# Layer 1 of the first mixture: both parts of the rows in one matmul of 448 columns, halves added on VectorE, ReLU and low part one block later

## The chip, the cores and the metric

The kernel runs on one core of a Trainium2 chip. The metric is the device time of one execution in microseconds (us). The kernel before took 871.7 us (median of 3 runs, 871.54 to 873.64).

## The reference

Attention over 4 batches, 12 heads, 448 positions and 64 dimensions gives 1792 rows of 768 numbers. Two mixtures of experts follow. The first gives each of its 8 experts exactly 224 rows; the second routes each row to its best expert with a gate weight.

```python
def _moe_ref(x, w_gate, w1, w2):
    N, D = x.shape                      # 1792, 768
    E = w_gate.shape[1]                 # 8 experts
    cap = N // E                        # 224 rows for each
    logits = x @ w_gate
    ...                                 # greedy assignment, best scores first, until an expert is full
    for e in range(E):
        mask = assigned == e
        h = np.maximum(x[mask] @ w1[e], 0.0)   # layer 1: 768 -> 1024
        out[mask] = h @ w2[e]                  # layer 2: 1024 -> 768
    return out
# the second mixture: e_idx = argmax(logits + bias of the row's modality),
# out[mask] = gate_w[mask, None] * (relu(x[mask] @ w1[e]) @ w2[e])
```

## The kernel before

All work is written out for one core in a fixed order: the instructions of each engine run in the order in which the program emits them, and semaphores make one engine wait for another. Attention fills about the first 245 us of the trace, the assignment of the first mixture the stretch up to about 290 us, and the experts the rest.

The experts are handled as tiles `u`. Tiles 0 to 7 are the experts of the first mixture, each 224 rows (two groups of 112). Tiles 8 and up belong to the second mixture, with 256 rows each (or 128 in a short one). Each matrix product is done in three parts so that rounded operands keep their accuracy: weights and rows are each split into an upper part and a low part (`wh`, `wl`, and `x[:, 0]`, `x[:, 1]`), and wh times upper, wh times low and wl times upper are summed in PSUM.

A tile is 16 chunks (`chunk(u, c)`). Chunks 0 to 7 are the 8 blocks of layer 1, 128 hidden units each: 6 slices of 128 input dimensions, and for each slice the three matmuls L1143 to L1145 of 224 columns, into one of three PSUM buffers `ph`. `layer1_end` then makes the ReLU on ScalarE (L1163, `hh`) and the low part on VectorE (L1164, `hl`), both from `ph`. Chunks 8 to 15 are layer 2 (L1177 to L1179, 384 columns each): chunk 8 uses blocks 0 to 3 of `hh` and `hl`, chunk 9 blocks 4 to 7, and so on for four outputs. A chunk has 12 of these matmuls; block 7 is first used by its 10th to 12th matmul in chunk 9, the 22nd to 24th of layer 2.

Within a chunk the order is: the matmuls of the layer; then what `run` finds in a table of work booked for that chunk (`at`); then the end of the layer; then work booked as late. Booked in the chunks of a tile of the first mixture are, among others:

- chunks 0 to 7: one slice each of the split of this tile's second weights (L815 on ScalarE makes the upper part, L817 on VectorE the low part, `w2s`, 768 columns);
- chunks 8 to 11: the splits of the next tile's first weights (`w1s`, 1024 columns), of which two stand in chunk 8, one in 9, two in 10 and one in 11;
- chunks 10 to 15: the transposes of the next tile's rows (L1120 to L1122);
- the routing of the tile before for the second mixture: transposes in chunks 0 and 1, logits in 2 (L1299, L1302), their sum in 3 (L1308, L1309), the choice in 4 (late, L1317 to L1323, six VectorE instructions and one of ScalarE), the placing in 6 (L1329 to L1345).

Tile 1 also has, in chunk 3, the sum of the lists of rows (L1254 to L1256), which waits for a load that follows a chain of scattering DMAs issued by GpSimd.

Of the kernel before, what the change touches and what calls it, by code (L numbers as in the profile page):

```python
# [8 lines left out]
FT = mybir.dt.float32  # L9
FR = mybir.dt.float32r  # L10
# [17 lines left out]
def build(ctx, tc, q, k, v, g_q, g_k, m1_gate, m1_w1, m1_w2, modality, m2_gate, m2_bias, m2_w1, m2_w2,  # L28
          out):
    nc = tc.nc  # L30
# [7 lines left out]
    E = m1_gate.shape[1]  # L38
    DJ = HD // 128
    F = m1_w1.shape[2]  # L40
    FB = F // 128
# [3 lines left out]
    T = 256  # L45
# [978 lines left out]
    with tc.If(f1 > 0):  # L1024
# [5 lines left out]
        with tc.If(f2 > 0):  # L1030
# [7 lines left out]
            with tc.If(f3 > 0):  # L1038
# [12 lines left out]
                hs = rr.tile([P, E], HF, name="hs")  # L1051
# [41 lines left out]


    act = ctx.enter_context(tc.tile_pool(name="act", bufs=1))
    HH, PY, LT2 = {}, {}, {}
    SHORT = set()
    bg = {}

# [3 lines left out]
    def run(w, late=False):  # L1103
        while bg.get((w, late)):
            f, a = bg[w, late].pop(0)
            f(*a)

    def shape(u):

        return (P, 2) if u < E else (128, 1) if u in SHORT else (128, 2)  # L1110
# [12 lines left out]

    def layer1(u, f):

        w, nt = shape(u)
        n = w * nt
        ph = ps1.tile([128, 512], FT, name="ph")
        o = slice(128 * f, 128 * f + 128)
        for j in range(DJ):  # L1130
            wh, wl = (W1S[u][:, i, j, o] for i in range(2))
            x = XS[u][:, j, :, :n]
            a, z = j == 0, j == DJ - 1
            if u == 0 and f == 0:

                for i in range(2):
                    nc.tensor.matmul(ph[:, :n], wh, x[:, i], start=(a and i == 0), stop=False)
                if z:
                    for k in range(DJ):
                        nc.tensor.matmul(ph[:, :n], W1S[u][:, 1, k, o], XS[u][:, k, 0, :n], start=False,  # L1140
                                         stop=(k == DJ - 1))
            elif nt == 2:
                nc.tensor.matmul(ph[:, :n], wh, x[:, 0], start=a, stop=False)  # L1143
                nc.tensor.matmul(ph[:, :n], wh, x[:, 1], start=False, stop=False)  # L1144
                nc.tensor.matmul(ph[:, :n], wl, x[:, 0], start=False, stop=z)  # L1145
            else:
                both = ph[:, :2 * n].rearrange("p (a n) -> p a n", a=2)
                nc.tensor.matmul(both, wh, x, start=a, stop=False)
                nc.tensor.matmul(both, wl, x, start=False, stop=z)
        return ph  # L1150

    def layer1_end(u, f, ph):
        w, nt = shape(u)
        n = w * nt
        if f == 0:
            HH[u] = [act.tile([128, FB, T], FR, name=nm) for nm in ("hh", "hl")]
        hh, hl = (x[:, f, :n] for x in HH[u])
        src = ph[:, :n]
        if nt == 1:
            src = act.tile([128, 128], FT, name="hs", bufs=2)  # L1160
            nc.scalar.activation(src, ph[:, n:2 * n], AF.Copy)
            nc.vector.tensor_add(src, ph[:, :n], src)
        nc.scalar.activation(hh, src, AF.Relu)  # L1163
        nc.vector.scalar_tensor_tensor(hl, src, 0.0, hh.bitcast(FT), op0=OP.max, op1=OP.subtract)  # L1164

    def layer2(u, i):
        w = shape(u)[0]
        t, s, z = i // 4, i // 2 % 2, i % 2
        if z == 0:
            PY[u] = ps2.tile([128, 512], FT, name="py")  # L1170
        hh, hl = HH[u]
        py = PY[u][:w, :384]
        o = slice(384 * s, 384 * s + 384)
        for f in range(4 * z, 4 * z + 4):
            wh, wl = (W2S[u][:, i, f, o] for i in range(2))
            a, b_ = (x[:, f, w * t:w * t + w] for x in (hh, hl))
            nc.tensor.matmul(py, a, wh, start=(f == 0), stop=False)  # L1177
            nc.tensor.matmul(py, b_, wh, start=False, stop=False)  # L1178
            nc.tensor.matmul(py, a, wl, start=False, stop=(f == FB - 1))  # L1179
# [20 lines left out]
    def chunk(u, c):  # L1200
        two = c >= 8 and c < 8 + 4 * shape(u)[1]
        if c < 8:
            ph = layer1(u, c)
        elif two:
            layer2(u, c - 8)
        run(16 * u + c)
        if c < 8:
            layer1_end(u, c, ph)
        elif two and c % 2:
            layer2_end(u, c - 8)  # L1210
        run(16 * u + c, True)

# [152 lines left out]
    took, cl, st, nt, ns, te, tb, one = (tq[:, i] for i in range(8))  # L1365
# [102 lines left out]
    for u in range(US):  # L1468
# [3 lines left out]
        for p in range(3, 7):  # L1472
            for i in range(2):
                c = 2 * (p - 3) + i
# [54 lines left out]
    for u in range(US):  # L1529
        for c in range(16):  # L1530
            chunk(u, c)
# [46 lines left out]
```

## Time and profile before

| | |
|---|---|
| median of 3 runs | 871.7 us (871.54 to 873.64) |
| the profiled execution | 873.17 us |
| its span, first to last instruction | 871.4 us |
| PE busy | 794.0 us, 91% of the span |
| VectorE (DVE) busy | 570.0 us, 65% |
| ScalarE (ACT) busy | 465.6 us, 53% |
| mean granted TensorE clock | 0.962 |

Times in the rows are microseconds from the start of the span. An instruction that overlaps its successor is counted at its full length in a mean, so the time from one start to the next (called a slot here) is shorter than the mean length: a row of the timeline gives a start, a length, and in brackets how long the engine was idle before it and who ended that. A granted clock of 1.00 is 2.4 GHz, 0.50 is 1.2 GHz.

The steady tiles of the first mixture are tiles 2 to 7; tile 2 starts layer 1 at about 371 us and layer 2 at 387.99 us.

### The profile page before, as it was taken

How to read it: one execution, taken by the hardware profiler on the slowest of the kernel's cores; microseconds unless marked ns; L12 is line 12 of the kernel's file. 1: busy time of each engine (PE TensorE's matmuls, PEld its weight loads, DVE VectorE, ACT ScalarE, POOL GpSimd, SP SyncE). 2: the span in 40 equal slices, each digit the busy share in tenths (PEclk: the TensorE clock that was granted, in tenths of full speed). 3: DMA queues.
4: the chain of work that ended last, by engine and by line, in shares of the span. 5: the costliest groups of instructions: out<-in, count | busy, mean ns of one | idle time of the engine just before them, and what ended most of it. 6: DMA issues, size and time to landing. Idle time of an engine off the chain costs nothing.

```text
span 871.4 us, 14927 instructions
## 1 busy us (share of the span) xinstructions
PE 794.0 (91%) x5630; PEld 653.5 (75%) x5630; DVE 570.0 (65%) x1196; ACT 465.6 (53%) x803; POOL 141.3 (16%) x230
## 2 busy tenths in 40 slices
PE   1589999999954998999999999999999999999994
PEld 1233333333343798999999999999999999999983
DVE  4899899894488954564746648475874565655641
ACT  3667767574361354554645546455564564555641
POOL 4440000000021344211101122121212010110000
PEclk9989999999965999999999999999999999999997
DMA  7349969774170695766757666485675775855710
GB/s 182 99 76 199 214 154 207 180 166 94 42 259 18 194 281 135 227 199 204 257 169 234 196 206 219 156 290 180 202 264 205 239 243 186 296 188 195 275 53 19
DMA packets 113785, 161.22 MB, mean 185 GB/s; under 512 B 59328, under 2 KB 77248, under 8 KB 113696
## 3 DMA queue, kind: packets, MB, share of 16 engines
q1 hardware_dynamic: 108928, 143.07, 55.7%
q0 software_dynamic: 4768, 17.02, 5.8%
q8 instruction: 49, 0.80, 0.4%
q14 instruction: 40, 0.33, 0.1%
HBM read 128.78 MB, written 17.22 MB: 168 GB/s over the span
## 4 chain that ended last, share of the span: by engine, by line
PE 52%; DMA 6%; issue 5%; DVE 1%; POOL 1%; SPq 0%; ACT 0%; POOLq 0%; DVEq 0%
PE py L1177 8%; PE py L1179 8%; PE py L1178 8%; PE ph L1143 8%; PE ph L1144 8%; PE ph L1145 8%; DMA l_d<-tok,p3i 4%; PE pt L1120 2%; DMA out_dram<-yr,lt 1%; PE pt L1289 1%; PE pi L1299 1%; DMA l<-l_d 1%; DMA lt<-l_d 0%; DVE w2s L817 0%; SPq L1250 0%
## 5 line engine op out<-in xcount | busy, mean ns | idle before, releaser
L1143 PE MATMUL ph<-xs,w1s 128*128 128x224 f32 (+1 forms) x714 | 201.4, 282 | 0.0
L1144 PE MATMUL ph<-xs,w1s 128*128 128x224 f32 (+1 forms) x714 | 197.1, 276 | 0.0
L1145 PE MATMUL ph<-xs,w1s 128*128 128x224 f32 (+1 forms) x714 | 197.0, 276 | 0.0
L1177 PE MATMUL py<-w2s,hh 128*112 128x384 f32 (+1 forms) x496 | 174.0, 351 | 1.4 <-ACT hh L1163 1.3
L1178 PE MATMUL py<-w2s,hl 128*112 128x384 f32 (+1 forms) x496 | 168.0, 339 | 0.0
L1179 PE MATMUL py<-w2s,hh 128*112 128x384 f32 (+1 forms) x496 | 167.9, 339 | 0.0
L817 DVE TENSOR_TENSOR w2s<-raw,w2s 128x768 fp32r<-128x768 f32 x128 | 122.5, 957 | 66.7 <-ACT w2s L815 66.6
L1143 PEld LDWEIGHTS ph<-xs,w1s 128*128 128x128 f32 x714 | 136.0, 190 | 2.9 <-DVE hl L1164 2.9
L1145 PEld LDWEIGHTS ph<-xs,w1s 128*128 128x128 f32 x714 | 136.2, 191 | 0.0
L1144 PEld LDWEIGHTS ph<-xs,w1s 128*128 128x128 f32 x714 | 136.2, 191 | 0.0
L817 DVE TENSOR_TENSOR w1s<-raw,w1s 128x1024 fp32r<-128x1024 f32 x96 | 113.3, 1221 | 16.4 <-ACT w1s L815 16.0
L815 ACT ACTIVATE w2s<-raw 128x768 fp32r<-128x768 f32 x128 | 107.3, 838 | 0.0
L1122 DVE TENSOR_TENSOR xs<-pt,xs 128x224 fp32r<-128x224 f32 (+2 forms) x92 | 36.6, 398 | 105.2 <-ACT xs L1121 105.2
L815 ACT ACTIVATE w1s<-raw 128x1024 fp32r<-128x1024 f32 x96 | 96.6, 1058 | 3.1 <-DVE lo L881 1.7
L1121 ACT ACTIVATE xs<-pt 128x224 fp32r<-128x224 f32 (+2 forms) x92 | 33.3, 362 | 112.5 <-PE pt L1120 86.6
L1177 PEld LDWEIGHTS py<-w2s,hh 128*112 128x112 f32 (+1 forms) x496 | 90.7, 183 | 2.3 <-ACT hh L1163 2.1
L438 ACT ACTIVATE pp<-sc,gs 128x896 f32<-128x896 f32 x72 | 70.0, 1006 | 41.1 <-PE sc L431 40.8
L1178 PEld LDWEIGHTS py<-w2s,hl 128*112 128x112 f32 (+1 forms) x496 | 90.8, 183 | 0.4
L1179 PEld LDWEIGHTS py<-w2s,hh 128*112 128x112 f32 (+1 forms) x496 | 90.4, 182 | 0.1
L1163 ACT ACTIVATE hh<-ph 128x224 fp32r<-128x224 f32 (+1 forms) x120 | 44.2, 368 | 78.6 <-PE ph L1145 76.2
L453 PE MATMUL av<-pp,vt 128*64 128x448 f32 x288 | 64.4, 554 | 0.0
L431 PE MATMUL sc<-qT,kT 128*128 128x448 f16 x144 | 53.1, 369 | 7.9 <-DVE qT L415 4.9
(321 smaller groups left out, 1087.0 us busy)
## 6 DMA issues: line engine op xcount, KB each, us to landing
raw<-in_moe_w_dram SPq DMA_DIRECT2D x48, 1024.0 KB, 4.9
raw<-in_moe_w_dram SPq DMA_DIRECT2D x64, 768.0 KB, 5.6
y_d<-yr SPq DMA_DIRECT2D x16, 336.0 KB, 3.8
qt<-in_q_dram SPq DMA_DIRECT2D x11, 448.0 KB, 5.2
kt<-in_k_dram SPq DMA_DIRECT2D x24, 192.0 KB, 3.6
vt<-in_v_dram SPq DMA_DIRECT2D x12, 384.0 KB, 4.5
qTs<-qT SPq DMA_DIRECT2D x20, 224.0 KB, 3.5
x_d<-xr SPq DMA_DIRECT2D x12, 336.0 KB, 3.0
```

The source lines that it names most:

```text
L431: nc.tensor.matmul(ps[:, s, :S], kT[:, 7 * j + 3 * s + g, :], rhs[s][z], start=(z == 0), stop=(z == 1))
L438: nc.scalar.activation(PP[n][:, 2 * g:2 * g + 2, :] if g < 3 else P7[n], ps[:, :w, :S], AF.Exp, scale=gs[:, 4:5])
L453: nc.tensor.matmul(AV[n][64 * s:64 * s + 64, :S], LV[u][:, 3 * (2 * j + s) + g, :], pp[:, 2 * g + s, :], start=(g == 0), stop=False, skip_ ...
L815: nc.scalar.activation(d[:, 0, j, c], RAW[u, p][:, i, c], AF.Copy)
L817: eng.tensor_sub(d[:, 1, j, c], RAW[u, p][:, i, c], d[:, 0, j, c].bitcast(FT))
L1143: nc.tensor.matmul(ph[:, :n], wh, x[:, 0], start=a, stop=False)
L1144: nc.tensor.matmul(ph[:, :n], wh, x[:, 1], start=False, stop=False)
L1145: nc.tensor.matmul(ph[:, :n], wl, x[:, 0], start=False, stop=z)
L1163: nc.scalar.activation(hh, src, AF.Relu)
L1177: nc.tensor.matmul(py, a, wh, start=(f == 0), stop=False)
L1178: nc.tensor.matmul(py, b_, wh, start=False, stop=False)
L1179: nc.tensor.matmul(py, a, wl, start=False, stop=(f == FB - 1))
```

## The change

For tiles of the first mixture (`u < E`) the two matmuls with the upper weights, which streamed 224 columns each into the same 224 columns of PSUM, become one that streams 448 columns into both halves of the buffer; the matmul with the low weights adds into the first half. The two halves then have to be added: ScalarE copies the second half into a new tile `hsum`, and VectorE adds the first half to it (`layer1_sum`). ReLU and low part read `hsum` in place of `ph`, and they are emitted one chunk later than before, ahead of the sum of the chunk's own block. The end of block 7 is thereby emitted in chunk 8. Tiles of the second mixture keep their order; a short one uses `hsum` where it had `hs`.

```diff
@@ layer1
             if u == 0 and f == 0:
-                for i in range(2):
-                    nc.tensor.matmul(ph[:, :n], wh, x[:, i], start=(a and i == 0), stop=False)
+                nc.tensor.matmul(ph[:, :2 * n].rearrange("p (a n) -> p a n", a=2), wh, x, start=a, stop=False,
+                                 skip_group_check=True)
...
+            elif u < E:
+                nc.tensor.matmul(ph[:, :2 * n].rearrange("p (a n) -> p a n", a=2), wh, x, start=a, stop=False,
+                                 skip_group_check=True)
+                nc.tensor.matmul(ph[:, :n], wl, x[:, 0], start=False, stop=z, skip_group_check=True)
             elif nt == 2:
@@ the end of a block
-    def layer1_end(u, f, ph):
+    def layer1_sum(u, f, ph):
...
         src = ph[:, :n]
-        if nt == 1:
-            src = act.tile([128, 128], FT, name="hs", bufs=2)
+        if u < E or nt == 1:
+            src = act.tile([128, T], FT, name="hsum", bufs=3)[:, :n]
             nc.scalar.activation(src, ph[:, n:2 * n], AF.Copy)
             nc.vector.tensor_add(src, ph[:, :n], src)
+        return src
+
+    def layer1_end(u, f, src):
+        w, nt = shape(u)
+        n = w * nt
+        hh, hl = (x[:, f, :n] for x in HH[u])
         nc.scalar.activation(hh, src, AF.Relu)
         nc.vector.scalar_tensor_tensor(hl, src, 0.0, hh.bitcast(FT), op0=OP.max, op1=OP.subtract)
@@ chunk
         run(16 * u + c)
-        if c < 8:
-            layer1_end(u, c, ph)
-        elif two and c % 2:
+        if u < E:
+            if 0 < c < 9:
+                layer1_end(u, c - 1, HS.pop())
+            if c < 8:
+                HS.append(layer1_sum(u, c, ph))
+        elif c < 8:
+            layer1_end(u, c, layer1_sum(u, c, ph))
+        if two and c % 2:
             layer2_end(u, c - 8)
```

On VectorE, around the end of layer 1 of a tile, the program before has this order (chunks 6 to 11; `w2s` and `w1s` are the low parts of weights, `hl` the low parts of blocks 6 and 7):

```order
L817 TENSOR_TENSOR w2s<-raw,w2s 128x768
L1164 SCALAR_TENSOR_TENSOR hl<-ph,hh 128x224
L817 TENSOR_TENSOR w2s<-raw,w2s 128x768
L1164 SCALAR_TENSOR_TENSOR hl<-ph,hh 128x224
L817 TENSOR_TENSOR w1s<-raw,w1s 128x1024 x5
```

The changed program has this there (L1175 is the low part, of blocks 5, 6 and 7, L1167 the sum of the halves, of blocks 6 and 7):

```order
L817 TENSOR_TENSOR w2s<-raw,w2s 128x768
L1175 SCALAR_TENSOR_TENSOR hl<-hsum,hh 128x224
L1167 TENSOR_TENSOR hsum<-ph,hsum 128x224
L817 TENSOR_TENSOR w2s<-raw,w2s 128x768
L1175 SCALAR_TENSOR_TENSOR hl<-hsum,hh 128x224
L1167 TENSOR_TENSOR hsum<-ph,hsum 128x224
L817 TENSOR_TENSOR w1s<-raw,w1s 128x1024 x2
L1175 SCALAR_TENSOR_TENSOR hl<-hsum,hh 128x224
L817 TENSOR_TENSOR w1s<-raw,w1s 128x1024 x3
```

The low part of block 7 has moved behind two splits of the next tile's first weights, and each block has one instruction more. On ScalarE the program before has, in chunks 6 to 9:

```order
L815 ACTIVATE w2s<-raw 128x768
L1163 ACTIVATE hh<-ph 128x224
L815 ACTIVATE w2s<-raw 128x768
L1163 ACTIVATE hh<-ph 128x224
L815 ACTIVATE w1s<-raw 128x1024 x3
```

and the changed program (L1174 is the ReLU, L1166 the copy of the second half):

```order
L815 ACTIVATE w2s<-raw 128x768
L1174 ACTIVATE hh<-hsum 128x224
L1166 ACTIVATE hsum<-ph 128x224
L815 ACTIVATE w2s<-raw 128x768
L1174 ACTIVATE hh<-hsum 128x224
L1166 ACTIVATE hsum<-ph 128x224
L815 ACTIVATE w1s<-raw 128x1024 x2
L1174 ACTIVATE hh<-hsum 128x224
L815 ACTIVATE w1s<-raw 128x1024
```

Here too the ReLU of block 7 has moved behind two upper parts of the next tile's first weights.

## Rows read from the trace of the kernel before

**Rows 1.** The page, part 1: busy time, share of the span, instructions.

```profile
PE 794.0 (91%) x5630; PEld 653.5 (75%) x5630; DVE 570.0 (65%) x1196; ACT 465.6 (53%) x803; POOL 141.3 (16%) x230
```

**Rows 2.** Waits of TensorE from 285 to 620 us: us in total, times, longest.

```profile
PE pi L1332 <- DVE d L1322: 2.6, 1, 2.6
```

**Rows 3.** Stretches: us, busy time of each engine, granted clock, DMA share, GB/s.

```profile
348.58:351.99 3.41, 3.41 (x16) 3.34 (x15) 3.17 (x13) 2.03 (x5) 0.96 (x1) 0.50 0.89 265
377.30:393.00 15.70, 15.70 (x129) 15.68 (x128) 12.91 (x31) 10.40 (x19) 2.23 (x3) 1.00 0.68 231
```

**Rows 4.** Timeline of TensorE, tile 2: start, length, line, tiles, shapes.

```profile
383.78 0.27 PE L1143 MATMUL ph<-xs,w1s 128*128 128x224 f32 x1
...
385.45 0.27 PE L1143 MATMUL ph<-xs,w1s 128*128 128x224 f32 x1
...
387.99 0.34 PE L1177 MATMUL py<-w2s,hh 128*112 128x384 f32 x1
...
390.94 0.34 PE L1179 MATMUL py<-w2s,hh 128*112 128x384 f32 x1
```

**Rows 5.** Timeline of TensorE in attention: scores of 448 columns.

```profile
108.97 0.35 PE L431 MATMUL sc<-qT,kT 128*128 128x448 f16 x1
...
110.29 0.35 PE L431 MATMUL sc<-qTs,kT 128*128 128x448 f16 x1
```

**Rows 6.** Timeline of VectorE, tile 2, chunks 2 to 8.

```profile
378.49 0.96 DVE L817 TENSOR_TENSOR w2s<-raw,w2s 128x768 fp32r<-128x768 f32 x1 [1.55 <-ACT w2s L815]
...
380.02 0.95 DVE L817 TENSOR_TENSOR w2s<-raw,w2s 128x768 fp32r<-128x768 f32 x1
380.89 0.39 DVE L1164 SCALAR_TENSOR_TENSOR hl<-ph,hh 128x224 fp32r<-128x224 f32 x1
381.19 0.95 DVE L817 TENSOR_TENSOR w2s<-raw,w2s 128x768 fp32r<-128x768 f32 x1
...
382.67 0.16 DVE L1317 TENSOR_REDUCE nm<-l 112x2 f32<-112x16 f32 x1
...
384.06 0.96 DVE L817 TENSOR_TENSOR w2s<-raw,w2s 128x768 fp32r<-128x768 f32 x1 [0.19 <-ACT w2s L815]
...
386.08 0.17 DVE L1336 TENSOR_TENSOR s<-pi,s 112x16 f32<-112x16 f32 x1 [0.70 <-PE pi L1335]
...
387.20 0.96 DVE L817 TENSOR_TENSOR w2s<-raw,w2s 128x768 fp32r<-128x768 f32 x1
...
389.25 0.39 DVE L1164 SCALAR_TENSOR_TENSOR hl<-ph,hh 128x224 fp32r<-128x224 f32 x1
389.55 3.49 DVE L817 TENSOR_TENSOR w1s<-raw,w1s 128x1024 fp32r<-128x1024 f32 x3
```

**Rows 7.** Groups of VectorE by shape: count, busy us, mean ns, idle before.

```profile
L1164 DVE SCALAR_TENSOR_TENSOR hl<-ph,hh 128x224 fp32r<-128x224 f32 x64 | 24.7, 385 | 2.6 <-ACT hh L1163 2.6
...
L1164 DVE SCALAR_TENSOR_TENSOR hl<-hs,hh 128x128 fp32r<-128x128 f32 x8 | 2.3, 292 | 3.0 <-ACT hh L1163 3.0
L1162 DVE TENSOR_TENSOR hs<-ph,hs 128x128 f32<-128x128 f32 x8 | 2.3, 283 | 0.0
```

**Rows 8.** Timeline of ScalarE, tile 2, chunks 7 to 9.

```profile
388.19 0.36 ACT L1163 ACTIVATE hh<-ph 128x224 fp32r<-128x224 f32 x1 [1.11 <-PE ph L1145]
388.44 2.95 ACT L815 ACTIVATE w1s<-raw 128x1024 fp32r<-128x1024 f32 x3
```

**Rows 9.** The page, part 5: the splits of first weights.

```profile
L817 DVE TENSOR_TENSOR w1s<-raw,w1s 128x1024 fp32r<-128x1024 f32 x96 | 113.3, 1221 | 16.4 <-ACT w1s L815 16.0
L815 ACT ACTIVATE w1s<-raw 128x1024 fp32r<-128x1024 f32 x96 | 96.6, 1058 | 3.1 <-DVE lo L881 1.7
```

**Rows 10.** The chain that ended last, tile 1: start, us, what.

```profile
344.88 0.96 DVE w2s L817
...
350.70 0.32 PE py L1177
351.02 0.32 PE py L1178
```

More of the change, by code (lines that the diff above doesn't have):

```diff
@@ L1095, in build @@
     act = ctx.enter_context(tc.tile_pool(name="act", bufs=1))
-    HH, PY, LT2 = {}, {}, {}
+    HH, PY, LT2, HS = {}, {}, {}, []
     SHORT = set()
@@ L1140, in layer1 @@
                         nc.tensor.matmul(ph[:, :n], W1S[u][:, 1, k, o], XS[u][:, k, 0, :n], start=False,
-                                         stop=(k == DJ - 1))
+                                         stop=(k == DJ - 1), skip_group_check=True)
+            elif u < E:
+                nc.tensor.matmul(ph[:, :2 * n].rearrange("p (a n) -> p a n", a=2), wh, x, start=a, stop=False,
+                                 skip_group_check=True)
+                nc.tensor.matmul(ph[:, :n], wl, x[:, 0], start=False, stop=z, skip_group_check=True)
             elif nt == 2:
@@ L1150, in layer1 @@
         return ph
-    def layer1_end(u, f, ph):
+    def layer1_sum(u, f, ph):
+        if f == 0:
+            HH[u] = [act.tile([128, FB, T], FR, name=nm) for nm in ("hh", "hl")]
         w, nt = shape(u)
         n = w * nt
-        if f == 0:
-            HH[u] = [act.tile([128, FB, T], FR, name=nm) for nm in ("hh", "hl")]
-        hh, hl = (x[:, f, :n] for x in HH[u])
         src = ph[:, :n]
-        if nt == 1:
-            src = act.tile([128, 128], FT, name="hs", bufs=2)
+        if u < E or nt == 1:
+            src = act.tile([128, T], FT, name="hsum", bufs=3)[:, :n]
             nc.scalar.activation(src, ph[:, n:2 * n], AF.Copy)
             nc.vector.tensor_add(src, ph[:, :n], src)
+        return src
[3 more added lines that the diff above has]
+        hh, hl = (x[:, f, :n] for x in HH[u])
         nc.scalar.activation(hh, src, AF.Relu)
```

## The prediction

> **What bounds the kernel now.** I read the page first, then the waits of TensorE over the stretch that the change touches, then the timelines of the three engines in one steady tile, and last the chain that ended last around tile 1. TensorE (PE) is busy for 91% of the span [rows 1]. In the tiles of the first mixture it is busier still: in the stretch of tile 2 from chunk 3 to chunk 9 it works 15.70 of 15.70 us at full clock [rows 3]. The one long wait from tile 0 to tile 7 is 2.6 us, where the placing in tile 1 waits for the choice on VectorE [rows 2]; VectorE had been held by the list load and starts again at 344.88 us [rows 10]. So from tile 2 on every TensorE slot that goes is time saved, if nothing else comes late. The reader is to see in the same row that VectorE is busy for 12.91 of these 15.70 us [rows 3]: it has 2.8 us left there, and the change gives it work in each block.
>
> **What goes from TensorE.** A matmul of 224 columns has a slot of 0.111 us (15 slots in 385.45 - 383.78 = 1.67 us), one of 384 columns 0.1735 us (17 slots in 2.95 us) [rows 4]. The pair that is merged cost 0.223 us. No row shows 448 columns of this type. The nearest below is the score of 448 columns in another type, 0.189 us (7 slots in 1.32 us) [rows 5]; the nearest above is the pair itself, 0.223 us. I take the rate of the 384-column row, 0.1735 x 448/384 = 0.202 us, since it is the same type and nearest in width. That saves 0.020 us a slice, and with 6 slices in 8 blocks 0.97 us a tile (nothing at the upper bound, 48 x 0.034 = 1.63 us at the lower). The matmul with the low weights stays at 0.111 us.
>
> The Trainium skill (TensorE: Matmul & The Clock Gate, sections Back-to-back issue gap and LDWEIGHTS) gives columns/2.4 + 2.5 ns at full clock, and columns of weights/1.2 for a weight load: 189 ns for 448 columns, 107 ns for a load of 128. The load would explain why 224 columns take 0.111 us and not 0.096, and the scores agree with 189 ns [rows 5], but for 384 columns it gives 162 ns where the trace has 173.5 [rows 4]. By the page the merged matmul would save 1.63 us a tile, the lower bound above.
>
> **What is added.** Per block one copy on ScalarE and one sum on VectorE. ReLU and low part change only their source. On VectorE the low part of 224 columns lasts 385 ns [rows 7] in a slot of 0.30 us (380.89 to 381.19) [rows 6]. In the short tiles, at 128 columns, the sum of halves lasts 283 ns and the low part that reads SBUF 292 ns [rows 7], so the two kinds cost about the same. I take 0.32 us as the slot of each. Bounds: 0.20 us (the 128-column lengths less the same overlap of 0.09), and 0.40 us (full length, no overlap). On ScalarE copy and ReLU take the slot of a ReLU, 0.25 us (388.19 to 388.44) [rows 8]; ScalarE has 5.3 us left in the stretch [rows 3] and 8 x 0.25 = 2 us are hidden there.
>
> **What is moved, and the sum for one steady tile.** The VectorE order sets when the low part of block 7 is ready, since it now stands behind two splits of the next first weights. I add up VectorE's queue in tile 2 on its own time axis. It idles 1.55 us before the low part of the second weights in chunk 2, at 378.49 us [rows 6]; there its queue is empty, and what it waits for follows TensorE. With three blocks shortened that start moves to 378.49 - 3/8 x 0.97 = 378.13. From there the queue holds:
>
> - six splits of second weights at a slot of 0.87 us (380.02 to 380.89): 5.22
> - six low parts (blocks 1 to 6) and six sums (blocks 2 to 7): 12 x 0.32 = 3.84
> - the choice with the short wait behind it, 382.67 to 384.06: 1.39; the placing, 386.08 to 387.20: 1.12; two small sums, about 0.2 [rows 6].
>
> That is 11.77 us, so the sum of block 7 leaves its slot at 389.90. The wait of 0.70 us ahead of the placing [rows 6] is gone, because VectorE arrives there late. Before, the low part of block 7 started at 389.25, 1.3 us after layer 2 had begun at 387.99 [rows 4, 6].
>
> Next the upper part of the next first weights on ScalarE: it stands behind ReLU 6, which needs the sum of block 6 (slot ends 389.90 - 1.51 = 388.39, result at 388.46), and the copy of block 7: two slots of 0.25, so it starts at 388.96 and lasts 1.06 us [rows 8, 9], to 390.02. VectorE starts its two splits then, at (3.49 - 1.22)/2 = 1.135 us each [rows 6, 9], and the low part of block 7 runs from 392.29 to 392.68. With the weight load that must follow it (one slot of 0.11) TensorE can go on at 392.8.
>
> TensorE wants it for the 23rd matmul of layer 2. Layer 2 begins 0.97 us earlier, at 387.02; 22 slots of 0.1735 make 390.84 [rows 4]. So TensorE waits 1.95 us, part of it one matmul earlier for the ReLU of block 7. Saved 0.97, lost 1.95: a steady tile gets 1.0 us longer. The gain hardly changes this: a faster merged matmul moves the start of VectorE's queue by 3/8 of the gain alone, so a tile loses 1.35 us if the merge saves nothing and 0.74 us if it saves 1.63. The VectorE slots count for more: 12 of them, so 0.40 us instead of 0.32 adds 0.96 us, and 0.20 takes 1.44 us off, which would make a tile 0.4 us shorter. Six such tiles (2 to 7): 6.0 us.
>
> **Tiles 0 and 1.** What tile 0 and blocks 0 to 6 of tile 1 save is covered by the 2.6 us wait [rows 2]: the list load, not TensorE, sets its end, so TensorE only waits longer; the same cover hides a wait for block 7 in tile 0. From 344.88 on [rows 10] VectorE has one more sum (and a low part of the same length as before) ahead of the choice, 0.34 us. Its queue up to the low part of block 7 is four splits with 0.64 us each of low part and sum (4 x 1.51 = 6.04), 1.39, 1.22, two splits 2.27 and 0.39: 356.2, with the weight load 356.3. TensorE began layer 2 at 350.70 with slots of 0.32 us [rows 10], at half clock until 351.99 [rows 3]: 4 slots there and 18 of 0.1735 make 355.1 before, 355.35 with the later choice and a block 7 that saves 0.1. It waits 0.95 us. Tile 1: 0.34 - 0.1 + 0.95 = 1.2 us.
>
> **The sum.** 6.0 + 1.2 = 7.2 us more. On the profiled execution, 873.17 us, that is 880.4; on the median of 871.7, which lies 1.5 us below it, 878.9. I predict 879.
>
> From tile 8 on nothing changes for the order, and TensorE is the bound there too, so what is lost before arrives at the end unchanged.
>
> **Rivals.**
>
> 1. The wait drops the clock. After the 2.6 us of idling in tile 1 TensorE ran at half clock for 3.41 us [rows 2, 3], which costs 1.7 us. The new wait of 1.95 us, in two parts with one matmul between, is nearly as long, and layer 2 behind it is bound by TensorE. If it happens in two to six of the seven tiles, 3.4 to 10 us come on top: 882 to 889, 886 in the middle. Against it: the new wait is shorter, and there is a matmul in it.
>
> 2. The queue on VectorE is shorter than I count, and the loss cancels the gain: 870 to 874. This needs about 0.9 us less up to block 7, slots of 0.25 us. For it: slots of 0.30 were seen [rows 6], and the small operations may fill gaps better. Against it: the splits alone take 5.22 + 2.27 us, and all of it was read from rows.
>
> 3. Faster. VectorE makes up its backlog, the low part of block 7 is ready by 390.84, and TensorE keeps the gain of the tiles 2 to 7: 6 x 0.97 = 5.8 us, 866. It decides where sum and low part together take about 0.31 us a block and not 0.64. The two instructions that this asks for at half their length have no row: the 128-column ones last 283 and 292 ns [rows 7], for little more than half of the columns.
>
> 4. The merge does not do what it says: 448 columns take as long as two times 224. Then a tile loses 1.35 us, 6 x 1.35 + 1.3 = 9.4 us, 881.
>
> **How the numbers follow.** The forecast, a wait at block 7 that outweighs the gain without a change of clock, 875 to 884: 60%. Rival 1: 17%, rival 2: 13%, rival 3: 6%, rival 4: 4%. No change means within 0.3% of 871.7, 869.1 to 874.3, about what a measurement of this kernel can tell. Slower takes the forecast with rivals 1 and 4, 81%; no change 13%; faster 6%. The range for 8 in 10 goes from the edge of rival 2 to the upper part of rival 1: 873.5 to 888. The forecast's own range, 875 to 884, comes from VectorE slots between 0.28 and 0.38 us.
>
> **What the profile after would show.** The matmul of 448 columns with a slot near 0.20 us. In each of the tiles 1 to 7 a wait of TensorE at L1188 and L1189 in chunk 9, put down to the ReLU L1174 (about 0.6 us) and the low part L1175 (about 1.3 us): some 13 us in all. VectorE without idle time from chunk 3 to the splits of first weights. Each of the tiles 2 to 7 about 1.0 us longer from one start of layer 1 to the next. The wait at the placing in tile 1 longer by 1 us or more, at no cost. Wrong would be: no wait in chunk 9 (then rival 3), a wait under 1 us (rival 2), half clock behind these waits (rival 1), or a new wait at a `ph` buffer or at the placing of a steady tile, which this sum does not have.

## The result and the profile after

The changed kernel took 884.2 us (median of 6 runs, 880.9 to 886.5), the kernel before 873.6 us beside it (6 runs, 871.5 to 874.0): a ratio of 1.0127, with a 95% interval of 1.0108 to 1.0146. That is 10.6 us more by the medians, 1.2%. The profiled execution of the changed kernel took 882.97 us, with a span of 881.2 us and a mean granted TensorE clock of 0.961.

The busy times of the engines (the page, part 1; columns as in [rows 1]) show the edit as it was described:

```profile
PE 792.7 (90%) x5246; PEld 640.6 (73%) x5246; DVE 589.6 (67%) x1260; ACT 483.1 (55%) x867; POOL 143.8 (16%) x230
```

TensorE issues 384 matmuls fewer than in [rows 1] (6 slices in 8 blocks in 8 tiles), VectorE 64 instructions more and ScalarE 64 more (one a block). Less work on TensorE, and a longer span: the time has to be in waits or in the clock. The waits of TensorE in the first mixture (line waited at, who ended it: us in total, times, longest) were one row of 2.6 us in [rows 2]. Now they are:

```profile
PE py L1189 <- DVE hl L1175: 6.7, 7, 1.1
PE pi L1349 <- DVE d L1339: 3.1, 1, 3.1
PE py L1188 <- ACT hh L1174: 2.8, 6, 0.6
```

The second row is the old wait of tile 1 at the placing. The other two are new: in each of the tiles 2 to 7 layer 2 stops at the ReLU of block 7 (0.41 to 0.56 us) and one matmul later at its low part (1.04 to 1.12 us). The seventh wait at L1189 is one of 0.32 us in tile 0; tile 1 has none in these rows. The timeline of TensorE at the turn from layer 1 to layer 2 in tile 2 (start, length, line, tiles and shapes; in brackets the idle time before and who ended it) shows three things:

```profile
385.98 0.38 PE L1144 MATMUL ph<-xs,w1s 128*128 128x448 f32 x1
386.20 0.26 PE L1146 MATMUL ph<-xs,w1s 128*128 128x224 f32 x1
386.30 0.33 PE L1188 MATMUL py<-w2s,hh 128*112 128x384 f32 x1
...
389.79 0.34 PE L1190 MATMUL py<-w2s,hh 128*112 128x384 f32 x1
390.67 0.42 PE L1188 MATMUL py<-w2s,hh 128*112 128x384 f32 x1 [0.54 <-ACT hh L1174]
392.14 0.52 PE L1189 MATMUL py<-w2s,hl 128*112 128x384 f32 x1 [1.05 <-DVE hl L1175]
392.46 0.52 PE L1190 MATMUL py<-w2s,hh 128*112 128x384 f32 x1
...
395.34 0.52 PE L1190 MATMUL py<-w2s,hh 128*112 128x384 f32 x1
395.66 0.39 PE L1188 MATMUL py<-w2s,hh 128*112 128x384 f32 x1
```

- The merged matmul has a slot of 0.22 us here (386.20 - 385.98) and the one behind it 0.10; over layer 1 of a tile the medians are 0.216 and 0.104 us. The gain is 0.80 us a tile: layer 1 of the tiles 2 to 7 takes 17.62 us, from its first matmul to that of layer 2, and took 18.42.
- The two waits cost 392.14 - 389.79 - 2 x 0.1735 = 2.00 us.
- Behind them the slots are 0.32 us (392.46 - 392.14) and not 0.1735, up to 395.66: TensorE runs at half clock (1.2 GHz).

The last point is seen at a glance in the stretches (us, busy time of each engine, granted clock, DMA share, GB/s; columns as in [rows 3]):

```profile
344.55:351.37 6.82, 6.25 (x24) 5.87 (x25) 6.15 (x22) 4.95 (x11) 2.09 (x2) 0.50 0.79 253
390.00:392.40 2.40, 0.81 (x3) 0.43 (x3) 2.40 (x4) 1.56 (x3) 2.25 (x4) 0.99 0.68 205
392.33:395.75 3.42, 3.42 (x12) 3.22 (x12) 2.17 (x3) 2.38 (x3) 1.47 (x5) 0.50 0.92 278
408.34:425.96 17.62, 17.62 (x125) 15.96 (x124) 11.63 (x35) 11.82 (x27) 1.96 (x2) 1.00 0.60 189
425.96:446.32 20.36, 18.89 (x117) 18.04 (x115) 11.92 (x18) 10.21 (x19) 5.22 (x9) 1.00 0.67 215
470.84:474.25 3.41, 3.41 (x13) 3.21 (x12) 2.43 (x3) 2.05 (x4) 0.97 (x7) 0.50 0.83 230
```

The clock was granted in full through the wait (second row) and halved behind it (third row), for 3.4 us; the same happened in tile 4 (last row). In tile 3 the same two waits left the clock at 1.00 through both layers (fourth and fifth rows), and so in tiles 5, 6 and 7. Half clock for 3.4 us costs 1.7 us (layer 2 takes 22.04 us in tile 2 and 20.36 in tile 3). In tile 1, behind the old wait at the placing, it lasted 6.82 us (first row), where it was 3.41 before [rows 3].

VectorE around the end of layer 1 in tile 2 (timeline, columns as for TensorE), to be laid beside [rows 6]:

```profile
377.29 0.96 DVE L817 TENSOR_TENSOR w2s<-raw,w2s 128x768 fp32r<-128x768 f32 x1 [1.15 <-ACT w2s L815]
378.16 0.38 DVE L1175 SCALAR_TENSOR_TENSOR hl<-hsum,hh 128x224 fp32r<-128x224 f32 x1
378.46 0.38 DVE L1167 TENSOR_TENSOR hsum<-ph,hsum 128x224 f32<-128x224 f32 x1
...
387.70 0.94 DVE L817 TENSOR_TENSOR w2s<-raw,w2s 128x768 fp32r<-128x768 f32 x1
388.56 0.38 DVE L1175 SCALAR_TENSOR_TENSOR hl<-hsum,hh 128x224 fp32r<-128x224 f32 x1
388.87 0.38 DVE L1167 TENSOR_TENSOR hsum<-ph,hsum 128x224 f32<-128x224 f32 x1
389.43 2.36 DVE L817 TENSOR_TENSOR w1s<-raw,w1s 128x1024 fp32r<-128x1024 f32 x2 [0.18 <-ACT w1s L815]
391.70 0.38 DVE L1175 SCALAR_TENSOR_TENSOR hl<-hsum,hh 128x224 fp32r<-128x224 f32 x1
```

The wait of 1.15 us before 377.29 is the last of any length (two of 0.18 us follow), and from there the queue is full; the sum of block 7 starts at 388.87, two splits of the next first weights come next, and only then the low part that TensorE wants. ScalarE (timeline) does the same with the ReLU:

```profile
388.11 0.34 ACT L1166 ACTIVATE hsum<-ph 128x224 f32<-128x224 f32 x1
388.34 1.99 ACT L815 ACTIVATE w1s<-raw 128x1024 fp32r<-128x1024 f32 x2
390.24 0.38 ACT L1174 ACTIVATE hh<-hsum 128x224 fp32r<-128x224 f32 x1
```

In [rows 8] the ReLU of block 7 ran ahead of these upper parts. The time of each stage of TensorE, from the first matmul of one layer to the first of the next:

| us | before | after |
|---|---|---|
| layer 1, each of tiles 2 to 7 | 18.42 | 17.62 |
| layer 2, tiles 3, 5, 6, 7 | 18.37 to 18.49 | 20.36 to 20.47 |
| layer 2, tiles 2 and 4 | 18.37 | 22.04, 22.07 |
| tiles 0 and 1, both layers | 78.13 | 79.27 |
| start of tile 2 to start of tile 8 | 220.87 | 231.53 |

So a steady tile loses 1.99 - 0.80 = 1.19 us; two of them lose 1.7 us more to the clock. With the 1.14 us of the tiles 0 and 1 this makes 6 x 1.19 + 1.14 + 3.4 = 11.7 us. The changed kernel had come to tile 0 2.04 us earlier in this execution, so tile 8 starts 9.77 us later than before. That start is not the edit's doing: it lies between 289.3 and 291.7 us in the ten profiled executions of this document, though no edit touches an instruction ahead of it. From tile 8 on nothing changes: the end of the span is 9.8 us later.

### The profile page after: what moved, and what is told of

It reads as the page before. It is cut to its first block, busy times and chain, and to the rows that moved or that the text cites. A ratio compares the mean times of both kernels' runs of the same rounds, so it can differ in the third digit from the quotient of the medians.

```text
span 881.2 us, 14323 instructions
## 1 busy us (share of the span) xinstructions
PE 792.7 (90%) x5246; PEld 640.6 (73%) x5246; DVE 589.6 (67%) x1260; ACT 483.1 (55%) x867; POOL 143.8 (16%) x230
## 4 chain that ended last, share of the span: by engine, by line
PE 62%; DVE 20%; DMA 7%; issue 5%; ACT 4%; POOL 1%; SPq 0%; DVEq 0%; ACTq 0%; POOLq 0%
PE py L1189 9%; PE py L1190 8%; PE py L1188 8%; PE ph L1148 4%; PE ph L1150 4%; PE ph L1149 4%; PE sc L431 4%; DVE w2s L817 4%; PE av L453 4%; DMA l_d<-tok,p3i 3%; PE ph L1144 3%; PE pt L1120 2%; ACT w2s L815 2%; PE av L447 2%; DVE hl L1175 1%
## 5 line engine op out<-in xcount | busy, mean ns | idle before, releaser
L1188 PE MATMUL py<-w2s,hh 128*112 128x384 f32 (+1 forms) x496 | 175.7, 354 | 4.2 <-ACT hh L1174 4.1
L1189 PE MATMUL py<-w2s,hl 128*112 128x384 f32 (+1 forms) x496 | 170.2, 343 | 6.7 <-DVE hl L1175 6.7
L1144 PE MATMUL ph<-xs,w1s 128*128 128x448 f32 x378 | 128.0, 390 | 0.0
L1146 PE MATMUL ph<-xs,w1s 128*128 128x224 f32 x378 | 101.0, 267 | 0.0
L1189 PEld LDWEIGHTS py<-w2s,hl 128*112 128x112 f32 (+1 forms) x496 | 91.6, 185 | 9.5 <-DVE hl L1175 8.9
L1188 PEld LDWEIGHTS py<-w2s,hh 128*112 128x112 f32 (+1 forms) x496 | 91.6, 185 | 7.5 <-ACT hh L1174 6.8
L1148 PE MATMUL ph<-xs,w1s 128*128 128x256 f32 x336 | 93.9, 280 | 0.0
L1150 PE MATMUL ph<-xs,w1s 128*128 128x256 f32 x336 | 92.9, 276 | 0.0
L1149 PE MATMUL ph<-xs,w1s 128*128 128x256 f32 x336 | 92.8, 276 | 0.0
L1190 PEld LDWEIGHTS py<-w2s,hh 128*112 128x112 f32 (+1 forms) x496 | 91.4, 184 | 0.3
L1144 PEld LDWEIGHTS ph<-xs,w1s 128*128 128x128 f32 x378 | 71.9, 190 | 8.7 <-DVE hl L1175 2.5
L1146 PEld LDWEIGHTS ph<-xs,w1s 128*128 128x128 f32 x378 | 73.2, 194 | 0.0
L1148 PEld LDWEIGHTS ph<-xs,w1s 128*128 128x128 f32 x336 | 63.1, 188 | 0.4 <-DVE hl L1175 0.4
```

The costliest lines, as they stand in the source:

```text
L1144: nc.tensor.matmul(ph[:, :2 * n].rearrange("p (a n) -> p a n", a=2), wh, x, start=a, stop=False, skip_group_check=True)
```

## The experiments

Two theories, both of which would give the waits above. *Position*: the end of block 7 is emitted behind the two splits of chunk 8, and that place alone makes it late. *Load*: sums and low parts are too much for VectorE beside the splits, wherever the end of block 7 stands. And a third question: whether the half clock comes from the two waits, and what it is worth. The kernels e1 to e4 ran on one chip (before: 873.9 us there), e5 to e8 on a second (before: 874.3 us). Each was run six times, e1 and e8 twelve times.

### e1: the end of block 7 ahead of the splits

```diff
         else:
             layer2(u, c - 8)
+        if u < E and c == 8:
+            layer1_end(u, 7, HS.pop())
         run(16 * u + c)
         if u < E:
-            if 0 < c < 9:
+            if 0 < c < 8:
                 layer1_end(u, c - 1, HS.pop())
```

> The changed kernel, but in chunk 8 the end of block 7 (ReLU and low part) is emitted ahead of the two splits of the next first weights. Theory A (the loss is the place of block 7's end behind two splits, 2.27 us of VectorE, and the clock drops that follow the wait): in tile 3 of the changed kernel the sum of block 7 ends at 428.80, so ReLU ends about 429.2 and the low part about 429.65, before TensorE wants it at 429.80: no wait in chunk 9, and each of the tiles 2 to 7 keeps the 0.7 to 0.8 us of layer 1: 867 to 870 where before takes 873, no half clock between 352 and 850 us. Rival B (VectorE's longer queue alone is too long, wherever the end of block 7 stands): a wait of 1 us or more stays, 876 to 880.

Measured: 869.6 us (867.5 to 872.4), a ratio of 0.9963 (0.9943 to 0.9983) to before. The same work as after, with two instructions in another place, is faster than before instead of slower. Its waits of TensorE in the first mixture:

```profile
PE pi L1351 <- DVE d L1341: 3.0, 1, 3.0
PE pt L1120 <- DVE xs L1122: 2.7, 2, 1.4
PE pt L1120 <- DMA xg<-x_d,idx: 1.7, 2, 1.4
```

No row for `hh` or `hl` is left. The timeline of VectorE in tile 3:

```profile
423.73 0.41 DVE L1175 SCALAR_TENSOR_TENSOR hl<-hsum,hh 128x224 fp32r<-128x224 f32 x1 [0.46 <-ACT hh L1174]
424.68 1.23 DVE L817 TENSOR_TENSOR w1s<-raw,w1s 128x1024 fp32r<-128x1024 f32 x1 [0.54 <-ACT w1s L815]
```

and the matmul of layer 2 that uses this low part (timeline of TensorE):

```profile
424.35 0.34 PE L1189 MATMUL py<-w2s,hl 128*112 128x384 f32 x1
```

The low part starts at 423.73 and lasts 0.41 us, so it is ready at 424.14, 0.2 us before its matmul; VectorE even waits 0.46 us for the ReLU ahead of it. Layer 2 of the tiles 2 to 5 takes 18.36 to 18.50 us, as before, and layer 1 keeps its 17.62. So sums and low parts are not too much for VectorE as such: under the same load, the place of block 7's end decides whether TensorE waits. The row at L1120 that waits for VectorE is what is late next: in tiles 6 and 7, where the choice of an expert for a tile of the second mixture (14 small instructions of VectorE) stands in chunk 9, layer 2 takes 19.96 and 20.06 us. With these two the tiles 2 to 7 together are 1.4 us shorter than before (219.47 against 220.87). The median is 4.3 us below that of before, and the traces, one of each kernel, don't show the edit making the rest.

### e2: the delay alone, without the merge

The three matmuls of before, no sum; ReLU and low part one chunk later, as in after.

```diff
         if u < E:
             if 0 < c < 9:
                 layer1_end(u, c - 1, HS.pop())
             if c < 8:
-                HS.append(layer1_sum(u, c, ph))
+                HS.append(ph)
```

> The kernel before with the order of the changed one: three matmuls of 224 columns and no sum, but ReLU and low part one block later, that of block 7 behind two splits in chunk 8. Theory A splits the wait of 1.5 us into order and longer queue: here the queue is short, the splits start at 389.3 and the low part ends near 392.0 where TensorE wants it at 391.8: a wait of 0.1 to 0.5 us a tile, 874 to 876. If the order alone makes the whole wait: 1.5 us a tile, 882 or more. Rival B (queue alone): 873, as before.

Measured: 882.6 us (879.6 to 884.6), ratio 1.01 (1.0069 to 1.0132). Waits of TensorE in the first mixture:

```profile
PE ph L1143 <- DVE hl L1164: 3.6, 2, 3.2
PE py L1178 <- DVE hl L1164: 1.9, 7, 0.3
```

The wait at block 7 is there in seven tiles, but 0.27 us long. A steady tile takes 18.57 + 18.93 us, 0.7 us more than before: 6 x 0.7 = 4.2 us. The first row stands in the tiles 0 and 1, where a `ph` buffer comes free a block later than before; it takes the place of the wait at the placing, and both tiles together take 80.8 us, 2.7 more than before. The time is that of the second theory (882 or more), but the wait at block 7 is that of theory A, so the order of the splits makes only a part of it. A third part was not expected: in the tiles 9 to 14, whose instructions stand in the old order, layer 1 takes 17.04 us where it took 16.41. The group of their first matmul, of 256 columns, in this kernel from 600 us on (count, busy us, mean ns, idle before):

```profile
L1143 PE MATMUL ph<-xs,w1s 128*128 128x256 f32 x328 | 92.7, 283 | 0.0
```

Its slot is 118 ns, 113.4 in the kernel before. What differs there are places in SBUF: `hh` and `hl`, which are allocated a chunk later, lie 2144 bytes higher, and four small tiles have changed places with them. From tile 8 to the start of tile 15 this kernel takes 248.08 us, and before, after and e1 take 243.47: 4.6 us. So the delay is tried again with the old places.

### e7: the delay alone, at the old places

```diff
-        if f == 0:
+        if f == 0 and u not in HH:
             HH[u] = [act.tile([128, FB, T], FR, name=nm) for nm in ("hh", "hl")]
...
+            if c == 0:
+                HH[u] = [act.tile([128, FB, T], FR, name=nm) for nm in ("hh", "hl")]
             if c < 8:
                 HS.append(ph)
```

> The delay alone once more (three matmuls, no sum, end of block 7 behind two splits), but hh and hl are taken from the pool in chunk 0 as in the kernel before, so that they lie at its addresses; in the run of the delay alone they lay 2144 bytes higher, and the slots of the 256-column matmuls of tiles 9 to 14, whose code did not change, were 118 ns and not 113.5. Theory E (the places in SBUF make these slots longer, 0.73 us a tile, 5 us in all): slots back at 113.5, the time at 876 to 878, and what the order alone costs is 0.5 to 0.7 us a tile. Rival (it belongs to the order or the build): slots at 118, 882.

Measured: 880.3 us (879.4 to 882.9), ratio 1.0092 (1.0064 to 1.0121). The slot of the 256 columns is 113.4 ns again, and the group (same columns) 279 ns:

```profile
L1143 PE MATMUL ph<-xs,w1s 128*128 128x256 f32 x328 | 91.5, 279 | 0.0
```

Layer 1 of the tiles 9 to 14 is back at 16.41 us, as theory E has it, but the time is above its 876 to 878. The steady tiles of the first mixture are as in e2: 18.57 + 18.92 us, with a wait of 0.28 us. So the later place alone costs 0.7 us a tile. Of that the wait takes 0.53 us in slots (the matmul that waits starts 0.62 us after the one before it and the next one 0.26 us later, where a slot is 0.1735), and 0.12 us stand in layer 1, at the last of four small matmuls of the routing's sum (219 ns to the next start, 99 before). The tiles 0 and 1 take 82.1 us, 3.9 more than before, again with waits for `ph`; the forecast had left them out. Without the sums VectorE reaches the splits earlier, and two splits in front of the low part cost little. The wait of 1.6 us of the changed kernel takes both: the queue that the sums fill, and the place behind the splits. With that place alone it is 0.3 us (e2, e7), with that queue alone there is none (e1).

### e3: the merge without the delay

```diff
         run(16 * u + c)
-        if u < E:
-            if 0 < c < 9:
-                layer1_end(u, c - 1, HS.pop())
-            if c < 8:
-                HS.append(layer1_sum(u, c, ph))
-        elif c < 8:
+        if c < 8:
             layer1_end(u, c, layer1_sum(u, c, ph))
```

> Merge and sum, but ReLU and low part in the same chunk, right behind the sum of the same block. Theory A: the low part of block 7 stands ahead of the splits, but each low part waits for copy, sum and ReLU of its own block, about 0.4 us of VectorE idling a block, which adds to the queue of 0.3 us sums: a wait in chunk 9 of 0 to 1.5 us a tile, 869 to 880, without the order of splits in it. Rival (the delay is what costs, the sum is free): 867 to 869.

Measured: 901.4 us (900.2 to 902.5), ratio 1.0321 (1.0292 to 1.035), 17 us worse than after and far outside the 869 to 880 of theory A. Waits of TensorE in the first mixture:

```profile
PE pi L1343 <- DVE d L1333: 13.3, 7, 3.0
PE py L1188 <- ACT hh L1174: 6.6, 7, 1.4
```

VectorE in tile 3 (timeline):

```profile
428.30 0.38 DVE L1167 TENSOR_TENSOR hsum<-ph,hsum 128x224 f32<-128x224 f32 x1
429.14 0.39 DVE L1175 SCALAR_TENSOR_TENSOR hl<-hsum,hh 128x224 fp32r<-128x224 f32 x1 [0.46 <-ACT hh L1174]
```

Sum, then ReLU on the other engine, then low part: VectorE idles 0.46 us in every block, the choice of the routing behind it comes late, and the placing waits in each of the tiles 1 to 7, 13.3 us in all. That is what the delay is there for. The second row is a wait at block 7 again, for its ReLU, though its end stands ahead of the splits: a queue that is long enough makes TensorE wait without the later place. The same kernel shows half clock in the tiles 1, 4, 5, 6 and 7.

### e4: the merge without the sum

As e3, but the second half of `ph` is not used; this leaves out the product of the upper weights with the low part of the rows.

```diff
         src = ph[:, :n]
-        if u < E or nt == 1:
+        if nt == 1:
```

> The merged matmul in the order of the kernel before, without copy and sum: ReLU and low part read the first half of the buffer, so the product of the upper weights with the low part of the rows is left out. It shows what the merge is worth alone. By the slots of the changed kernel (0.320 us for the pair of 448 and 224 columns, three of 224 take 0.334) 0.7 to 0.8 us for each of the tiles 2 to 7, nothing for tiles 0 and 1: 4 to 5 us less than before, 868 to 869, no wait in chunk 9. Rival C (merging is no gain, since what follows is late anyway): as before.

Measured: 865.9 us (865.2 to 869.6), ratio 0.9912 (0.9885 to 0.994): 8.0 us less than before. Layer 1 takes 17.62 us in all steady tiles and layer 2 18.36 (18.50 in tile 7), and the only wait on VectorE is that of tile 1 (waits of TensorE):

```profile
PE pi L1343 <- DVE d L1333: 5.4, 1, 5.4
```

So the merge is worth 6 x 0.80 = 4.8 us in the steady tiles, if the sum were free. The profiled execution, 869.6 us, was the longest of the six, and what makes up the other 3 us of the median can't be read from it; the forecast had 868 to 869.

### e5: dummy matmuls in the waits

As after, with three matmuls of 384 columns, into a buffer that nobody reads, ahead of the matmul that needs `hh` of block 7, and six ahead of the one that needs `hl`.

```diff
+    def keep_busy(u, n):
+        pw = ps1.tile([128, 512], FT, name="ph")
+        for _ in range(n):
+            nc.tensor.matmul(pw[:P, :384], HH[u][0][:, 0, :P], W2S[u][:, 0, 0, :384], start=True, stop=True)
...
+            if u < E and i == 1 and f == FB - 1:
+                keep_busy(u, 3)
             nc.tensor.matmul(py, a, wh, start=(f == 0), stop=False)
+            if u < E and i == 1 and f == FB - 1:
+                keep_busy(u, 6)
             nc.tensor.matmul(py, b_, wh, start=False, stop=False)
```

> The changed kernel with nine extra matmuls of 384 columns a tile of the first mixture, into a PSUM buffer that nobody reads: three ahead of the first matmul that needs block 7's ReLU, six ahead of the one that needs its low part. They stand where TensorE waits 0.4 and 1.05 us, and take 0.5 and 1.05 us. Theory A (part of the loss is half clock that follows the waits, 3.4 us of it twice in the profiled execution, 1.7 us each): no half clock between 380 and 640 us, tiles 2 to 7 all 1.2 to 1.4 us longer than before, the time 880 to 882 and its spread over the runs under 3 us where the changed kernel had 5.6. Rival (the clock would fall anyway, or the extra matmuls cost their full 1.56 us on top of the wait): half clock as before or 890 and more.

Measured: 881.9 us (880.8 to 883.5), ratio 1.0103 (1.0075 to 1.013). Stretch from tile 2 to tile 8 in this kernel:

```profile
380.00:640.00 260.00, 259.94 (x1716) 244.50 (x1709) 170.98 (x424) 149.25 (x306) 45.27 (x70) 1.00 0.63 205
```

and in the changed kernel:

```profile
380.00:640.00 260.00, 250.81 (x1638) 235.67 (x1637) 168.76 (x417) 146.80 (x300) 45.78 (x71) 0.99 0.63 201
```

TensorE has no waits left in this stretch and the clock is 1.00 throughout. Each layer 2 of the tiles 2 to 7 takes 20.31 to 20.48 us: the wait itself stays (it is filled, not removed), and the 22 us of tiles 2 and 4 are gone. The kernel is 7.6 us slower than its own before, after was 10.6; the intervals of the two ratios overlap, and the traces show two stretches of 1.7 us less.

The spread of the runs says nothing here: those of e5 lie within 2.8 us and those of after within 5.6, but the 17 runs of before beside e5 lie within 7.8 us without these waits. The clocks of the runs say more. Every run has a span and a mean granted clock, and span x (1 - clock) estimates the time that the missing clock cost (3.4 us at half clock count 1.7). Its median is 36.2 us for after, 32.5 for e5 and 33.1 for the 17 runs of before. That is 3.7 us more in after than in e5, about the two stretches, though the clock is noted to 0.001 only (0.9 us of a span) and single runs overlap (32.5 to 39.8 against 30.8 to 34.4). The other profiles agree: in the tiles 2 to 7 half clock appears only in the three kernels that have two or more waits in each of these tiles, in two tiles of after, in four of e3 and in five of e6. The other seven kernels have none there, e1 not even behind its single waits of 1.4 and 1.3 us.

### e6: two splits on GpSimd

As after, but two of the eight low parts of second weights run on GpSimd, to shorten VectorE's queue.

```diff
-                at(u, c, w_split, u, p, i, nc.vector)
+                at(u, c, w_split, u, p, i, nc.gpsimd if u < E and c in (3, 5) else nc.vector)
```

> The changed kernel, but in tiles of the first mixture the low parts of the second weights of chunks 3 and 5 are made on GpSimd: two slots of 0.87 us less in VectorE's queue, the order of all else as it is. Theory A (order and queue together make the wait: a short queue leaves 0.27 us of it, as the run with the delay alone shows): the wait in chunk 9 falls from 1.5 to 0.3 us or less a tile, 868 to 872. Theory D (the order alone makes it): still 1.5 us, 884. Unknown is how long GpSimd takes for 768 columns; block 3 and 5 of layer 2 are due 8 to 12 us later, so up to 4 us each would be hidden.

Measured: 906.6 us (902.1 to 906.8), ratio 1.0387 (1.0356 to 1.0417), far worse, and outside both forecasts. The queue got longer: TensorE's waits at L1188 and L1189, 9.5 us in after, come to 19.1. GpSimd in tile 3 (timeline):

```profile
425.73 1.84 POOL L817 TENSOR_TENSOR w2s<-raw,w2s 128x768 fp32r<-128x768 f32 x1 [25.58 <-PE pi L1325]
...
430.95 1.84 POOL L817 TENSOR_TENSOR w2s<-raw,w2s 128x768 fp32r<-128x768 f32 x1 [0.84 <-ACT w2s L815]
```

VectorE beside it (timeline):

```profile
426.44 1.38 DVE L1175 SCALAR_TENSOR_TENSOR hl<-hsum,hh 128x224 fp32r<-128x224 f32 x1 [0.38 <-ACT hh L1174]
...
431.18 1.86 DVE L1175 SCALAR_TENSOR_TENSOR hl<-hsum,hh 128x224 fp32r<-128x224 f32 x1 [0.45 <-ACT hh L1174]
```

A low part that lasts 0.38 us alone lasts until 0.25 us after the end of GpSimd's split (427.57 to 427.82, and 432.79 to 433.04). Two splits of 0.87 us left VectorE's queue, and 1.00 + 1.48 us of stretching and 0.83 us of waits for the ReLU came in. The Trainium skill (SBUF — State Buffer, Who interferes with whom) says that a VectorE instruction with two SBUF inputs contends with a GpSimd instruction that reads SBUF, that the ports they share are an exclusive lock, and that the order of issue decides who blocks. The trace agrees with both ends above, where GpSimd had started first; in tiles 0 and 7 the low part started 0.07 and 0.03 us ahead of the split and was held until 0.25 us or less behind its end all the same.

The low part reads `hsum` and `hh`, both in SBUF; in the kernel before it read `ph`, in PSUM, and `hh`. No run puts a split on GpSimd beside a low part that reads `ph`, but a small instruction of GpSimd shows the difference. It starts while the low part of block 7 runs, in e2 (first row, low part from `ph`) and in after (second row, low part from `hsum`; timelines of GpSimd):

```profile
356.50 0.21 POOL L1275 TENSOR_TENSOR sb<-inf,bias 112x16 f32<-112x16 f32 x1
391.81 0.35 POOL L1287 TENSOR_TENSOR sb<-inf,bias 112x16 f32<-112x16 f32 x1
```

Beside the low part that reads `hsum` it lasts 0.35 us and not 0.21. As a test of the load this experiment decides nothing, since it raised the load.

### e8, the best version: end of block 7 first, the choice later

As e1, and the choice for a tile of the second mixture moves from chunk 9 to chunk 14.

```diff
-            at(u, 9, tile_pick, u - E + 2, late=True)
+            at(u, 14, tile_pick, u - E + 2, late=True)
```

> As the run with the end of block 7 ahead of the splits, and the picking of the second mixture's first tiles (some 14 small VectorE instructions, late in chunk 9 of tiles 6 and 7) moved to late in chunk 14. In that run layer 2 of tiles 6 and 7 took 19.96 and 20.06 us and not 18.37, with waits of TensorE's transposes L1120 for VectorE's low part L1122. Theory F (the picking stands in a VectorE queue that the sums made 1 us later): both waits go, 18.4 us, the time 3 us under that run: 866 to 867. Rival: the waits move elsewhere, 869 to 870.

Measured: 868.9 us (866.2 to 871.4), ratio 0.9941 (0.9921 to 0.9961), 5.4 us faster than before. Waits of TensorE in the first mixture:

```profile
PE pi L1351 <- DVE d L1341: 5.5, 1, 5.5
PE pt L1120 <- DMA xg<-x_d,idx: 2.1, 1, 2.1
```

The time lies between the forecast (866 to 867) and its rival (869 to 870). The waits for VectorE at the transposes are gone; layer 2 of the tiles 6 and 7 takes 18.37 and 18.52 us. Both rows that are left lie in the tiles 0 and 1, and from 368 to 600 us TensorE is busy for all of it (stretch, columns as above):

```profile
368.00:600.00 232.00, 232.00 (x1551) 219.13 (x1550) 151.75 (x354) 139.18 (x292) 52.87 (x67) 1.00 0.66 206
```

Against e1 the gain is 0.7 us of median between two chips, which the intervals don't tell apart; that the two tiles are 1.6 and 1.5 us shorter is read from the traces. The tiles 2 to 7 together take 216.39 us, 4.5 less than before.

## Why the prediction was right and wrong

The direction, the place of the new waits and the queue that makes them were right. The time, 884.2 us, lies in the range for 8 in 10 (873.5 to 888) and 0.2 us beyond the forecast's own, 875 to 884. The loss was 10.6 us where the sum had 7.2. **The step that failed is the clock behind the new waits**: the sum took it at nothing and gave it to rival 1 with 17%, "Against it: the new wait is shorter, and there is a matmul in it." Neither helped. Waits of 0.54 and 1.05 us with one matmul between were followed by half clock in two of the six steady tiles, 2 x 1.7 = 3.4 us; "half clock behind these waits (rival 1)" was one of the prediction's own signs of being wrong, and 884.2 lies in rival 1's 882 to 889. With the 0.2 us that each tile lost beyond its forecast the six tiles come to 10.5 us, not 6.0. Dummy matmuls in the waits (e5) took the half clock away and left the rest of the loss standing. The predicted time is off by 5.2 us: about 3.4 us of it are this term, and the kernel before took 1.9 us more in the runs beside the changed one than in the three that were shown. A second term had the right size by luck, that of the tiles 0 and 1 below.

Point by point:

- *The merge saves 0.97 us a tile.* It saves 0.80. The merged slot is 0.216 us and not 0.202, near the upper bound; the slot behind it is 0.104 and not 0.111. By the Trainium skill's columns/2.4 + 2.5 ns (TensorE: Matmul & The Clock Gate, Back-to-back issue gap), which the page gives for an isolated matmul, it would be 189 ns, and the measurement decides against it for this type. Rival 4 is out too.
- *VectorE's queue.* It was to restart at 378.13 on the time axis of before, which is 0.89 us ahead of that of after at this point (tile 2 starts layer 1 at 369.57 us before, not at about 371, and at 368.68 after), hence 377.24, and to hold 11.77 us up to the end of block 7's sum. It restarts at 377.29 and the sum leaves its slot at 389.17, after 11.88 us. That is closer than its parts: the slots of sum and low part were 0.30 and not 0.32 us (378.16 to 378.46), and the placing with the small sums took 1.58 us where the prediction had 1.32, which nearly cancels. The group rows (columns as in [rows 7]) show the nearly equal lengths that were taken from the short tiles:

```profile
L1175 DVE SCALAR_TENSOR_TENSOR hl<-hsum,hh 128x224 fp32r<-128x224 f32 x64 | 24.9, 389 | 0.0
L1167 DVE TENSOR_TENSOR hsum<-ph,hsum 128x224 f32<-128x224 f32 x64 | 24.5, 382 | 0.0
```

- *The wait.* 1.95 us forecast, 2.00 us of slots lost in tile 2; idle time of 0.6 and 1.1 us at most, in the order and by the releasers that were named. The rows add up to 9.5 us and not to some 13, since tile 1 is missing and the idle time that the profile names, 1.6 us a tile, is less than the slots that are lost.
- *A steady tile.* 1.0 us forecast, 1.19 without the clock: all of the difference is the smaller gain.
- *Tiles 0 and 1.* 1.2 us forecast, 1.14 measured, and the agreement is luck. The sum had a wait of 0.95 us at block 7 in tile 1. There the low part's matmul starts 0.33 us after the one before it, and the next one 0.27 us later (timeline of TensorE, tile 1):

```profile
353.70 0.34 PE L1188 MATMUL py<-w2s,hh 128*112 128x384 f32 x1
354.03 0.43 PE L1189 MATMUL py<-w2s,hl 128*112 128x384 f32 x1
```

Two slots of 0.1735 us are 0.35, so block 7 costs 0.25 us. In its place stands half clock of 6.82 us and not 3.41, which costs 1.7 us more and brings TensorE later to block 7. From the point where VectorE starts again after the list load (342.39 us, 344.88 before [rows 10]) tile 2 is 26.29 us away and was 24.69.

- *The wait at the placing in tile 1* was to be longer by 1 us or more; it was 0.5 us longer (3.1 against 2.6). By itself it costs nothing, since the lists set its end; whether the longer half clock behind it comes from these 0.5 us is not shown (in e1 3.41 us followed a wait of 3.0).
- *Rivals 2 and 3* needed a shorter queue or a low part in time. Rival 3 is what e1 makes true, not by faster VectorE instructions, as the rival had it, but by their place.

What stays open: why the half clock follows the waits in tiles 2 and 4 and not in 3, 5, 6 and 7, where the same waits stand; why it lasted twice as long in tile 1; and what the places in SBUF do to the slots in e2.

## What to carry to other kernels

When a result that is made late is wanted early by the engine that bounds the kernel, emit its last piece ahead of the work that is booked for the same stretch: moving two instructions here turned a loss of 10.6 us into a gain of 4.3 (medians, each against its own before). When a change makes the bounding engine TensorE wait in short pieces, put half clock behind them into the sum with its price, not only among the rivals: here it was a third of the loss. When a predicted term agrees, look whether its cause is there too: the 1.2 us of the tiles 0 and 1 were another 1.14. And an operand that moves from PSUM to SBUF can change what the instruction contends with, so a helper engine may cost more than it takes over, as in e6.

## What the runs showed of the hardware

- Half clock (0.50) for 3.4 us followed waits of 1.6 us in all that were split by one matmul, in two tiles of six of the changed kernel; with matmuls that do nothing in the waits (e5) it followed in none.
- The slot of the same 256-column matmul was 118 or 113.4 ns, in all of the tiles 9 to 14, by where `hh` and `hl` lay in SBUF (2144 bytes apart), which these matmuls neither read nor write (four small tiles lay elsewhere too). It made the tiles 8 to 14 4.6 us longer in the profiled executions of e2 and e7; the medians, each against its own before, are 2.7 us apart (8.7 and 6.0). The two ran on different chips, but e1 and e4, on the chip of e2, have 113 ns. Two builds show it, and the mechanism is open.
- A 448-column matmul of this type had a slot of 0.216 us and the 224-column one behind it 0.104, where 224 columns behind 224 take 0.111.
- A GpSimd subtraction of 768 columns took 1.84 us, 0.96 on VectorE, and held up VectorE's low parts until it was done: their mean went from 389 ns in the changed kernel to 675 in e6.
- A GpSimd instruction of 0.21 us beside a VectorE instruction that reads PSUM and SBUF (e2) took 0.35 us beside one that reads SBUF twice (after).
